# From the tenth tile on: attention scores in 64x32 sub-arrays without masked blocks, and the state's output of even and odd heads side by side

## The chip, the cores and the metric

One NeuronCore of one Trainium2 chip runs the whole program. TensorE does the matmuls (it writes PSUM, which has eight banks), VectorE, ScalarE and GpSimd do element-wise work, SyncE issues most DMAs. The metric is the device time of one execution in microseconds; the time before is the median of three runs, 780.83 us (778.70 to 780.98).

## The reference

Three parts in a row, for 4 batches, 8 heads, 768 steps and head size 48. First a linear attention with a decaying state, for each batch and head:

```
cur   = outer(u * k[t], v[t])
y[t]  = r[t] @ (state + cur)
state = w[t][:, None] * state + outer(k[t], v[t])
```

Its output, 3072 tokens of 384 features (8 heads of 48), goes through a feed-forward layer of width 2048, `(h * clip(h + 3, 0, 6) / 6) @ w_out` with `h = x @ w_in`, and then through a second one of width 1024, whose middle is `h * softmax(h)` followed by a normalisation. All inputs are float32.

## The kernel before, in words

Attention is cut into 24 tiles: 6 groups of 128 steps times 4 batches. Within a tile the recurrence is written as matmuls: running products of w (`q` backwards, `e` forwards) scale k and r. The scores of a tile are 128x128 for each head; only the part with the key's step before the query's step counts. The diagonal is replaced by `d`, the sum of r, k and u over the head. A tile goes through five stages, each with a function:

- `stw` clips w. `st0` brings w and r to the layout "head features on partitions" and builds `q` and `e`. `st1` does the same for k and multiplies r, k and u on GpSimd. From tile 10 (`LATE`) the turning is done by VectorE (`flip`, L438) from tiles that the DMA has laid out (`load_late`); before, TensorE does it.
- `st2` (L554 to L576) turns the scaled keys back (`ktp`, copied to `ktok`), computes the scores (`pa0` for even heads, whose 48 features lie on partitions 0 to 47, `pa1` for odd heads, on partitions 64 to 111), and makes `am`: GpSimd writes the diagonal (L572), VectorE copies the scores in where the mask `causal` says so (L576).
- `st3` (L585 to L639) computes the addition to the state (`kv`), then the tile's output `yt`: `inter` (L600) is scaled r times the decayed state `sp` or `sr`, `intra` (L607) is scores times v. Four matmuls of 32 output columns stand beside each other in the array. Features are stored as three chunks of 128: chunk c < 2 holds features 0 to 31 of heads 4c to 4c+3, chunk 2 the features 32 to 47 of all heads. VectorE adds `kv` to the state (L626), ScalarE and VectorE split the output into two float32r parts, `xh` (L638) and `xl` (L639).

The first feed-forward layer runs group by group, in 96 slots (6 groups times 16 blocks of its width). Slot n does `ffn_in(n)` (L657, nine matmuls into `h`), then the attention stages that are due, then `ffn_out(n - 2)` (L677, nine matmuls into three banks that are kept for the group). Each product is three float32r matmuls (hi*hi, hi*lo, lo*hi). ScalarE and VectorE do the function between (L661 to L665). `sched` sets the slots: for tile i from 10 on, with 4(i-4) as base, stages `stw` to `st2` stand in slots base-5 to base-2 and `st3` in base+2. So `st2` of tile i+1 and `st3` of tile i fall into the same slot, `st2` first. The second layer (L872 to L902) follows when the first is done.

PSUM: pool `ps_h` has two banks, for `h` and, from tile 9 on, `kv`; `ps_y` has three, for the feed-forward's sum; `ps_a` has three, through which the turned w, r, k, `ktp`, `pa0`, `pa1` and `yt` rotate (`ps_tile`). The order on SyncE is written out by hand; that of the other engines is set by a planner, which goes by program order and by when it thinks that operands and buffers are ready. Each engine then works in that order, and waits on semaphores.

Of the kernel before, what the change touches and what calls it, by code (L numbers as in the profile page):

```python
# [8 lines left out]
F32 = mybir.dt.float32  # L9
BF16 = mybir.dt.bfloat16  # L10
F32R = mybir.dt.float32r
I32 = mybir.dt.int32
# [6 lines left out]
P = 128  # L19
# [259 lines left out]
def fast_path(  # L279
# [70 lines left out]
    ps_a = right.enter_context(tc.tile_pool(name="ps_a", bufs=3, space=PSUM, side="right"))  # L350

    WN = KD * P + DM
    w1_h = w1p.tile([P, M1, WN], F32R, name="w1_h")
# [3 lines left out]
    def w1_load(m):  # L357
        ms = slice(m * P, (m + 1) * P)
        t = dec.tile([P, WN, 2], I32, tag="raw", name="raw", bufs=3)
        rows = w_in1[:, 2 * m * P:2 * (m + 1) * P]  # L360
        lo = t[:, 0:2 * P, :].rearrange("p (c f) w -> p c (f w)", c=2)
        src = rows.rearrange("(c q e) f -> c q e f", c=2, e=D)
# [46 lines left out]

    def late_open():  # L410
        pool = right.enter_context(tc.tile_pool(name="late", bufs=1, side="right"))
        for nm in ("w", "r", "k"):
# [3 lines left out]
            late[nm] = t  # L416

    def load_late(i):

        g, b = divmod(i, B)  # L420
        at[i] = {}
        for nm, src in (("w", w), ("r", r), ("k", k)):
            x = src[b].rearrange("(hp two) (n p j) d -> two n p hp (j d)", two=2, n=NG, j=4)
            for par in range(2):
                for half in range(2):
                    lo, n = 32 * half, 4 * D - 16 - 16 * half
                    o = 64 * par + lo
                    nc.sync.dma_start(out=late[nm][o:o + 32, :, 0:n], in_=x[par, g, :, :, lo:lo + n])
        for nm, src in (("r", r), ("k", k)):
            t = inp.tile([P, H, D], F32, tag=nm, name=nm)  # L430
            nc.sync.dma_start(out=t, in_=src[b, :, g * C:(g + 1) * C, :].rearrange("h t d -> t h d"))
            at[i][nm] = t
        load_v(i)

    def flip(nm):

# [5 lines left out]
        return t  # L442

    def ps_tile(nm):
        return ps_a.tile([P, 4, P], F32, tag="pa", name=nm)

    def ps_in(i, nm, spare):
        if i >= B:
# [94 lines left out]
        )  # L543
        a["sp"], a["sr"] = sp, sr

    def st2(i):
        a = at[i]
        g = i // B
        kq = a["q"][:, :, 1:C + 1]
        rr = a["e"]  # L550
        if g < NG - 1:
            ktp = ps_tile("ktp")
            for hp in range(HP):
                nc.tensor.transpose(out=ktp[:, hp, 0:DP], in_=kq[0:DP, hp, :], identity=ident[0:DP, 0:DP])  # L554
            ktok = atp.tile([P, HP, DP], F32, tag="ktok", name="ktok")
            nc.scalar.activation(out=ktok, in_=ktp[:, :, 0:DP], func=ACTF.Copy)
            a["ktok"] = ktok
        a["am"] = []
        pas = [ps_tile("pa0"), ps_tile("pa1")]
        d = atp.tile([P, H], F32, tag="d", name="d")  # L560
        nc.vector.tensor_reduce(out=d, in_=a["z"], axis=AX.X, op=ALU.add)
        for j in range(HP):
            for hh, pa in enumerate(pas):
                o = 64 * hh
                nc.tensor.matmul(
                    out=pa[:, j, :], lhsT=kq[o:o + D, j, :], rhs=rr[o:o + D, j, :], start=True, stop=True
                )
        dv = d.rearrange("p (j hh) -> p hh j", hh=2)
        for hh, pa in enumerate(pas):
            am = atp.tile([P, 4, C], F32, tag="am", name="am")  # L570
            a["am"].append(am)
            nc.gpsimd.tensor_tensor(  # L572
                out=am, in0=ident.unsqueeze(1).to_broadcast([P, HP, C]),
                in1=dv[:, hh, :].unsqueeze(2).to_broadcast([P, HP, C]), op=ALU.mult,
            )
            nc.vector.copy_predicated(am, causal.unsqueeze(1).to_broadcast([P, HP, C]), pa)  # L576

    def st3(i):
        a = at[i]
        g, b = divmod(i, B)  # L580
        if g < NG - 1:
            kv = ps_tile("kv") if i < JOIN - 1 else ps_h.tile([P, HP, P], F32, tag="h", name="kv")
            for h in range(H):
                o = 64 * (h % 2)
                nc.tensor.matmul(  # L585
                    out=kv[o:o + D, h // 2, 0:D], lhsT=a["ktok"][:, h // 2, o:o + D], rhs=a["v"][:, h, :],
                    start=True, stop=True, skip_group_check=True,
                )
        y = ps_tile("yt")

        def inter(c, first):
            for q in range(4):
                if c < 2:
                    h = 4 * c + q
                    hp, f = h // 2, D * (h % 2)
                    lhs = a["sp"][0:DP, hp, f:f + 32]
                else:
                    hp = q
                    lhs = a["sr"][0:DP, q, :]
                nc.tensor.matmul(  # L600
                    out=y[32 * q:32 * q + 32, c, :], lhsT=lhs, rhs=a["e"][0:DP, hp, :], start=first, stop=not first,
                    skip_group_check=True,
                )

        def intra(c, heads, lo, n, first, last):
            for q, h in enumerate(heads):
                nc.tensor.matmul(  # L607
                    out=y[32 * q:32 * q + n, c, :], lhsT=a["v"][:, h, lo:lo + n], rhs=a["am"][h % 2][:, h // 2, :],
                    start=first, stop=last, skip_group_check=True,
                )  # L610

        for c in range(2):
            if g > 0:
                inter(c, True)
            intra(c, range(4 * c, 4 * c + 4), 0, 32, g == 0, True)
        intra(2, range(1, H, 2), 16, 32, True, False)
        intra(2, range(0, H, 2), 32, 16, True, g == 0)
        if g > 0:
            inter(2, False)
        if g < NG - 1:  # L620
            for j in range(2):
                o, f = 64 * j, D * j
                dst = s_st[b][o:o + D, :, f:f + D]
                src = kv[o:o + D, :, 0:D]
                if g > 0:
                    nc.vector.tensor_tensor(out=dst, in0=src, in1=a["sp"][o:o + D, :, f:f + D], op=ALU.add)  # L626
                else:
                    nc.scalar.activation(out=dst, in_=src, func=ACTF.Copy)
        at.pop(i)
# [7 lines left out]
        xf = y[:, 0:KD, :]  # L637
        nc.scalar.activation(out=xh[:, :, sl], in_=xf, func=ACTF.Copy, accum_out=chk[:, 3 * i + 2:3 * i + 3])  # L638
        nc.vector.tensor_tensor(out=xl[:, :, sl], in0=xf, in1=xh[:, :, sl].bitcast(F32), op=ALU.subtract)  # L639

    stages = [stw, st0, st1, st2, st3]

# [50 lines left out]
    def range_a():  # L693

        xs = chk[:, 0:3 * NTILE].rearrange("p (n c) -> p n c", c=3)[:, :, 2]
        nc.vector.tensor_scalar(out=xs, in0=xs, scalar1=0.0, scalar2=None, op0=ALU.mult)
# [118 lines left out]
    for n in range(NSLOT + LAG):  # L815
        if n < NSLOT:
            ffn_in(n)
        for i, s in sorted(sched.get(n, []), key=lambda x: (x[0] - 2 * (x[0] >= JOIN and x[1] == 3), x[1])):
            stages[s](i)
            if s == NS - 1 and JOIN <= i + 1 < NTILE:  # L820
# [13 lines left out]
        if n == M1:  # L834
            dec_st.close()
            late_open()
        if n == NA:
# [127 lines left out]
```

## Time and profile before

| | |
|---|---|
| median of 3 runs | 780.83 us |
| the profiled execution | 780.79 us |
| its span in the profile | 779.1 us |
| TensorE matmul busy | 736.6 us (95%) |
| VectorE, ScalarE, GpSimd busy | 531.6, 333.6, 262.0 us |

The profile is of one execution. Busy time counts the time in which an engine has at least one instruction under way; TensorE's matmuls overlap, so the sum of their durations is larger than their share of the time, and what one costs in a run is read from the distance between starts. The page counts an fp32 matmul as two matmul instructions and a float32r matmul as one.

### The profile page before, as it was taken

What the parts mean: (1) busy time and instruction counts of PE and PEld (TensorE: products, weight loads), DVE (VectorE), ACT (ScalarE), POOL (GpSimd) and SP (SyncE); (2) the same over time, 40 slices, a digit from 0 to 9 for tenths busy, and PEclk for the clock granted to TensorE, in tenths of its full rate; (3) what the DMA queues carried; (4) which work ended last, traced back from release to release, by engine and by line L of the source; (5) the groups of instructions that cost most, each with busy time, mean ns of one, the idle gap of its engine ahead of it and who ended that gap; (6) DMA issues with size and microseconds to landing.
All of it is one profiled execution on the core that took longest, in us unless ns stands there. A gap on an engine that the chain in (4) does not pass through costs nothing. (4 is left out here: it accounts for less than half of the span.)

```text
span 779.1 us, 13589 instructions
## 1 busy us (share of the span) xinstructions
PE 736.6 (95%) x5084; PEld 621.3 (80%) x5084; DVE 531.6 (68%) x1010; ACT 333.6 (43%) x647; POOL 262.0 (34%) x355
## 2 busy tenths in 40 slices
PE   6669798999999999999999999999999999999996
PEld 4547676888888888888888887877889999999996
DVE  6989889667677777777778856886565555555552
ACT  3455555334444334433344335654444344333442
POOL 5566647642333233333233211232222222222200
PEclk8889997999999999999999999999999999999999
DMA  9785653514345333433334003440111111111001
GB/s 172 176 167 138 163 131 97 108 41 86 84 85 126 84 84 85 125 85 85 85 89 120 1 1 104 145 133 26 61 42 42 51 41 41 48 45 42 31 20 36
DMA packets 139435, 64.79 MB, mean 83 GB/s; under 512 B 90848, under 2 KB 133984, under 8 KB 139360
## 3 DMA queue, kind: packets, MB, share of 16 engines
q1 hardware_dynamic: 136768, 59.11, 32.2%
q10 hardware_dynamic: 2592, 4.72, 1.6%
q8 instruction: 42, 0.69, 0.4%
q14 instruction: 33, 0.27, 0.1%
HBM read 54.37 MB, written 9.44 MB: 82 GB/s over the span
## 5 line engine op out<-in xcount | busy, mean ns | idle before, releaser
L677 PE MATMUL y<-gh,w_h 128*128 128x512 f32 x288 | 116.7, 405 | 1.0 <-ACT ye L683 1.0
L657 PE MATMUL h<-xh,w_h 128*128 128x512 f32 x288 | 113.0, 393 | 3.0 <-DVE t L662 2.9
L677 PE MATMUL y<-gl,w_h 128*128 128x512 f32 x288 | 114.0, 396 | 0.0
L677 PE MATMUL y<-gh,w_l 128*128 128x512 f32 x288 | 113.4, 394 | 0.0
L657 PE MATMUL h<-xl,w_h 128*128 128x512 f32 x288 | 112.8, 392 | 0.0
L657 PE MATMUL h<-xh,w_l 128*128 128x512 f32 x288 | 112.5, 391 | 0.0
L661 ACT ACTIVATE t<-h,cols 128x512 f32<-128x512 f32 x96 | 65.3, 681 | 104.9 <-PE h L657 101.8
L663 ACT ACTIVATE gh<-t 128x512 fp32r<-128x512 f32 x96 | 60.5, 630 | 103.7 <-DVE t L662 103.5
L662 DVE SCALAR_TENSOR_TENSOR t<-t,h 128x512 f32<-128x512 f32 x96 | 65.4, 681 | 41.2 <-ACT t L661 41.0
L665 DVE TENSOR_TENSOR gl<-t,gh 128x512 fp32r<-128x512 f32 x80 | 66.8, 835 | 36.0 <-ACT gh L663 35.0
L78 DVE TENSOR_REDUCE nm<-h 128x1 f32<-128x1024 f32 x24 | 29.4, 1226 | 61.5 <-PE h L872 61.4
L899 PE MATMUL po<-w_oh,qh 128*128 128x384 f32 x192 | 67.1, 350 | 0.3 <-ACT qh L888 0.3
L657 PEld LDWEIGHTS h<-xh,w_h 128*128 128x128 f32 x288 | 54.4, 189 | 16.0 <-DVE t L662 4.2
L677 PEld LDWEIGHTS y<-gh,w_h 128*128 128x128 f32 x288 | 54.7, 190 | 15.5 <-issue 3.2
L899 PE MATMUL po<-w_oh,ql 128*128 128x384 f32 x192 | 64.7, 337 | 0.1
L899 PE MATMUL po<-w_ol,qh 128*128 128x384 f32 x192 | 64.8, 337 | 0.0
L677 PEld LDWEIGHTS y<-gh,w_l 128*128 128x128 f32 x288 | 54.9, 191 | 11.8
L677 PEld LDWEIGHTS y<-gl,w_h 128*128 128x128 f32 x288 | 55.0, 191 | 11.0 <-DVE gl L665 0.6
L657 PEld LDWEIGHTS h<-xh,w_l 128*128 128x128 f32 x288 | 54.4, 189 | 11.3
L657 PEld LDWEIGHTS h<-xl,w_h 128*128 128x128 f32 x288 | 54.4, 189 | 11.2
L888 ACT ACTIVATE qh<-pt 128x512 fp32r<-128x512 f32 x48 | 26.1, 597 | 78.3 <-PE pt L886 78.3
L872 PE MATMUL h<-w_ih,yl 128*128 128x512 f32 x144 | 56.4, 391 | 0.0
(123 smaller groups left out, 1478.7 us busy)
## 6 DMA issues: line engine op xcount, KB each, us to landing
raw<-in_moe_w_out_dram SPq DMA_DIRECT2D x24, 384.0 KB, 5.9
raw<-in_moe_w_in_dram SPq DMA_DIRECT2D x48, 128.0 KB
r<-in_r_dram SPq DMA_DIRECT2D x24, 192.0 KB
k<-in_k_dram SPq DMA_DIRECT2D x24, 192.0 KB, 3.7
v<-in_v_dram SPq DMA_DIRECT2D x24, 192.0 KB, 4.0
y1d<-ye ACTq DMA_DIRECT2D x18, 256.0 KB, 2.3
y<-y1d SPq DMA_DIRECT2D x24, 192.0 KB, 2.8
out_dram<-os SPq DMA_DIRECT2D x24, 192.0 KB, 1.9
```

The source lines that it names most:

```text
L78: nc.vector.tensor_reduce(out=nm, in_=h, axis=AX.X, op=ALU.max, negate=True)
L657: nc.tensor.matmul(out=h, lhsT=a, rhs=b, start=(j == 0), stop=(j == len(ops) - 1))
L661: nc.scalar.activation(out=t, in_=h, func=ACTF.Relu, bias=three)
L662: nc.vector.scalar_tensor_tensor(out=t, in0=t, scalar=6.0, in1=h, op0=ALU.min, op1=ALU.mult)
L663: nc.scalar.activation(out=gh, in_=t, func=ACTF.Copy)
L665: eng.tensor_tensor(out=gl, in0=t, in1=gh.bitcast(F32), op=ALU.subtract)
L677: nc.tensor.matmul(out=y_ps[g][c], lhsT=a, rhs=b, start=(m == 0 and j == 0), stop=(m == M1 - 1 and j == 2))
L872: nc.tensor.matmul(out=h[:, fs], lhsT=a[:, c, :], rhs=b_[:, c, fs], start=(j == 0), stop=(j == len(ops) - 1))
L888: nc.scalar.activation(out=qh[:, ms, :], in_=pt, func=ACTF.Copy)
L899: nc.tensor.matmul(out=po, lhsT=x[:, m, :], rhs=y[:, m, :], start=(n == 0), stop=(n == 3 * M2 - 1))
```

## The change

The scores leave `st2`: `keys_in` (turning the keys) stays there, while from tile 10 (`JOIN`) on `scores(i + 1)` is called in `st3(i)`, between the state addition and the output of tile i, so that the scores stand next to the part of the output that has the same array shape.

```
        else:
            mask, diag = late["mask"], late["diag"]
            d0 = d
            d = late["v"].tile([P, H], F32, tag="dt", name="dt")
            nc.gpsimd.tensor_copy(out=d[:, 0:4], in_=d0[:, 0:4])
            for o, n, t0 in turned:
                nc.gpsimd.tensor_copy(out=d[o:o + n, 4:8], in_=d0[t0:t0 + n, 4:8])
            for j in (0, 2, 1, 3):
                for x in range(4):
                    ks = 32 * x
                    for hh, pa in enumerate(pas):
                        o, p = 64 * hh, ks if j < 2 else 96 - ks
                        nc.tensor.matmul(
                            out=pa[p:p + 32, j, ks:C], lhsT=kq[o:o + D, j, ks:ks + 32], rhs=rr[o:o + D, j, ks:C],
                            start=True, stop=True, skip_group_check=True,
                        )
```

Each head's 128 keys are cut into four blocks of 32, and block x is multiplied only with the queries from step 32x on: 128, 96, 64 and 32 columns. For the head pairs j = 2 and 3 the blocks are stored in reversed order of partitions. So the mask, the diagonal, `d` and v are needed in that order for these heads: mask and diagonal are loaded once (`late_mask`), v once more for each tile in five DMAs (`load_turned`, tile `vt`), `d` by five small GpSimd copies.

```
+            mask, diag = (x.unsqueeze(1).to_broadcast([P, HP, C]) for x in (causal, ident))
...
+    turned = [(32 * q, 32, 96 - 32 * q) for q in range(4)]
+        for hs, parts in ((slice(0, 4), [(0, P, 0)]), (slice(4, 8), turned)):
+            for o, n, t0 in parts:
+                nc.sync.dma_start(out=t[o:o + n, hs, :], in_=src[hs, t0:t0 + n, :].rearrange("h t d -> t h d"))
```

The output's chunks 0 and 1 now hold features 0 to 31 of the even and of the odd heads (for all tiles; the rows of the feed-forward's weights are loaded in that order). From tile 10 on `inter` of chunk 0 takes 48 rows from partition 0, of chunk 1 48 rows from partition 64, both at the head, and chunk 1 goes to a bank of its own from `ps_h`:

```
+        if i >= JOIN:
+            y1 = ps_h.tile([P, C], F32, tag="h", name="yt1")
+            ys[1] = y1
...
+                    if i >= JOIN:
+                        rows = slice(64 * c, 64 * c + D)
+                    lhs = a["sp"][rows, q, D * c:D * c + 32]
...
+        if i >= JOIN:
+            inter(0, True)
+            inter(1, True)
...
+                (slice(1, 2), ys[1].unsqueeze(1), late["tot"][:, i:i + 1]),
+                (slice(0, KD, 2), y[:, 0:KD:2, :], chk[:, 3 * i + 2:3 * i + 3]),
```

`xh` and `xl` of these tiles are each made in two instructions. PSUM is divided anew in slot 22: `ps_a` is closed, two banks become `pa0` and `pa1` for good (cleared once, since the masked blocks are never written), one bank serves the turned w, r, k and `yt`. `ktp` of tiles from 10 on goes to `ps_h`, which then serves `h`, `ktp`, `kv` and `yt1`.

```
+    def ps_late():
+        ps_st.close()
+        pool = right.enter_context(tc.tile_pool(name="ps_s", bufs=1, space=PSUM, side="right"))
+        late["pa"] = [pool.tile([P, HP, C], F32, name=f"late_pa{j}") for j in range(2)]
+        for t in late["pa"]:
+            nc.vector.memset(t, 0.0)
+        late["one"] = right.enter_context(tc.tile_pool(name="ps_one", bufs=1, space=PSUM, side="right"))
...
+        if n == 4 * (JOIN - B) - 2:
+            ps_late()
+        if n >= max(LAG, 4 * (JOIN - B) - 2):
+            ffn_out(n - LAG)
         for i, s in sorted(sched.get(n, []), key=lambda x: (x[0] - 2 * (x[0] >= JOIN and x[1] == 3), x[1])):
...
-        if n >= LAG:
+        if LAG <= n < 4 * (JOIN - B) - 2:
             ffn_out(n - LAG)
```

So from slot 22 on `ffn_out` stands between `ffn_in` and the attention stages. In `st3` VectorE's additions to the state come ahead of the output, for all tiles.

## Rows read from the trace of the kernel before

**Rows 1.** The page: busy us (share of the span) and instructions.
```profile
PE 736.6 (95%) x5084; PEld 621.3 (80%) x5084; DVE 531.6 (68%) x1010; ACT 333.6 (43%) x647; POOL 262.0 (34%) x355
```
**Rows 2.** Stretches: length, busy of each engine, granted clock, DMA share, GB/s.
```profile
120.00:140.00 20.00, 17.33 (x76) 13.81 (x75) 16.64 (x28) 8.26 (x16) 13.22 (x12) 0.81 0.41 86
140.00:160.00 20.00, 20.00 (x170) 16.49 (x170) 12.88 (x25) 8.88 (x16) 13.72 (x20) 1.00 0.38 82
...
300.00:320.00 20.00, 20.00 (x165) 16.64 (x164) 14.44 (x29) 7.80 (x15) 6.44 (x8) 1.00 0.38 82
...
480.00:500.00 20.00, 19.03 (x85) 15.42 (x84) 15.61 (x27) 13.69 (x31) 5.55 (x6) 1.00 0.47 145
```
**Rows 3.** Waits of TensorE, 200 to 480 us: total us, times, longest.
```profile
PEld y L677 <- issue: 2.8, 14, 0.2
PEld pa L565 <- issue: 1.4, 4, 0.4
```
**Rows 4.** TensorE in order of time: start us, length us, operation, count.
```profile
300.59 0.39 PE L677 MATMUL y<-gh,w_h 128*128 128x512 f32 x1
...
304.67 0.39 PE L677 MATMUL y<-gh,w_h 128*128 128x512 f32 x1
...
306.71 0.39 PE L657 MATMUL h<-xh,w_h 128*128 128x512 f32 x1
...
308.52 0.40 PE L657 MATMUL h<-xh,w_l 128*128 128x512 f32 x1
308.76 0.55 PE L554 MATMUL ktp<-ident,q 112*128 112x112 f32 x4
309.23 1.16 PE L565 MATMUL pa<-e,q 48*128 48x128 f32 x16
310.32 0.56 PE L585 MATMUL kv<-v,ktok 128*48 128x48 f32 x16
310.82 0.42 PE L600 MATMUL yt<-e,sp 112*32 112x128 f32 x8
311.06 0.41 PE L607 MATMUL yt<-am,v 128*32 128x128 f32 x8
...
312.16 0.41 PE L600 MATMUL yt<-e,sr 112*32 112x128 f32 x8
312.50 0.50 PE L677 MATMUL y<-gh,w_h 128*128 128x512 f32 x1
312.83 0.40 PE L677 MATMUL y<-gl,w_h 128*128 128x512 f32 x1
```
**Rows 5.** The same view, from 310.815 to 310.85 us alone.
```profile
310.82 0.32 PE L600 MATMUL yt<-e,sp 112*32 112x128 f32 x4
```
**Rows 6.** Stretches (columns of rows 2): kv, and the output.
```profile
310.32:310.82 0.50, 0.50 (x18) 0.44 (x17) 0.10 (x1) 0.36 (x1) 0.00 (x0) 1.00 0.00 0
310.82:312.50 1.68, 1.68 (x61) 1.48 (x57) 1.33 (x4) 0.27 (x1) 0.00 (x0) 1.00 0.00 0
```
**Rows 7.** VectorE in order of time, about the same tile.
```profile
309.74 0.69 DVE L662 SCALAR_TENSOR_TENSOR t<-t,h 128x512 f32<-128x512 f32 x1 [0.95 <-ACT t L661]
...
311.73 0.72 DVE L626 TENSOR_TENSOR s_st<-kv,sp 48x192 f32<-48x192 f32 x2
...
316.10 0.54 DVE L639 TENSOR_TENSOR xl<-yt,xh 128x384 fp32r<-128x384 f32 x1
```
**Rows 8.** ScalarE in order of time.
```profile
309.60 0.54 ACT L556 ACTIVATE ktok<-ktp 128x448 f32<-128x448 f32 x1
```
**Rows 9.** GpSimd in order of time; in brackets the idle time before, and its cause.
```profile
312.59 0.84 POOL L535 TENSOR_TENSOR sp<-s_st,q 112x384 f32<-112x384 f32 x1 [2.95 <-PE yt L600]
...
315.39 0.41 POOL L539 TENSOR_TENSOR sr<-s_st,q 112x128 f32<-112x128 f32 x1
315.86 0.11 POOL L498 MEMSET q<- 112x4 f32 x1
```
**Rows 10.** The page: DMA issues, KB each, median us from issue to landing.
```profile
v<-in_v_dram SPq DMA_DIRECT2D x24, 192.0 KB, 4.0
```

More of the change, by code (lines that the diff above doesn't have):

```diff
@@ L349, in fast_path @@
     dec = dec_st.enter_context(tc.tile_pool(name="dec", bufs=2, side="right"))
-    ps_a = right.enter_context(tc.tile_pool(name="ps_a", bufs=3, space=PSUM, side="right"))
+    ps_st = ExitStack()
+    ps_a = ps_st.enter_context(tc.tile_pool(name="ps_a", bufs=3, space=PSUM, side="right"))
     WN = KD * P + DM
@@ L416, in late_open, with late_mask, load_turned @@
             late[nm] = t
+        late["tot"] = pool.tile([P, NTILE], F32, name="late_tot")
+        nc.gpsimd.memset(late["tot"], 0.0)
+        late["mask"] = pool.tile([P, HP, C], I32, name="late_mask")
+        late["diag"] = pool.tile([P, HP, C], F32, name="late_diag")
+    def late_mask(nm, src):
+        for hs, parts in ((slice(0, 2), [(0, P, 0)]), (slice(2, 4), turned)):
+            for o, n, t0 in parts:
+                nc.sync.dma_start(
+                    out=late[nm][o:o + n, hs, :], in_=src[t0:t0 + n, :].unsqueeze(1).to_broadcast([n, 2, C])
+                )
+    turned = [(32 * q, 32, 96 - 32 * q) for q in range(4)]
+    def load_turned(t, src):
+        for hs, parts in ((slice(0, 4), [(0, P, 0)]), (slice(4, 8), turned)):
+            for o, n, t0 in parts:
+                nc.sync.dma_start(out=t[o:o + n, hs, :], in_=src[hs, t0:t0 + n, :].rearrange("h t d -> t h d"))
     def load_late(i):
@@ L432, in load_late @@
             at[i][nm] = t
-        load_v(i)
+        if g < NG - 1:
+            load_v(i)
+        t = late["v"].tile([P, H, D], F32, tag="vt", name="vt")
+        load_turned(t, v[b, :, g * C:(g + 1) * C, :])
+        at[i]["vt"] = t
     def flip(nm):
@@ L544, in state_in, with keys_in @@
         a["sp"], a["sr"] = sp, sr
-    def st2(i):
+    def keys_in(i):
         a = at[i]
-        g = i // B
+        if i // B == NG - 1:
+            return
+        kq = a["q"][:, :, 1:C + 1]
+        ktp = ps_tile("ktp") if i < JOIN else ps_h.tile([P, HP, P], F32, tag="h", name="ktp")
+        for hp in range(HP):
+            nc.tensor.transpose(out=ktp[:, hp, 0:DP], in_=kq[0:DP, hp, :], identity=ident[0:DP, 0:DP])
+        ktok = atp.tile([P, HP, DP], F32, tag="ktok", name="ktok")
+        nc.scalar.activation(out=ktok, in_=ktp[:, :, 0:DP], func=ACTF.Copy)
+        a["ktok"] = ktok
@@ L549, in st2, with scores @@
+    def scores(i):
+        a = at[i]
         kq = a["q"][:, :, 1:C + 1]
         rr = a["e"]
[L551 to L557, printed above, removed]
         a["am"] = []
-        pas = [ps_tile("pa0"), ps_tile("pa1")]
+        pas = [ps_tile("pa0"), ps_tile("pa1")] if i < JOIN else late["pa"]
@@ L560, in st2 @@
         d = atp.tile([P, H], F32, tag="d", name="d")
         nc.vector.tensor_reduce(out=d, in_=a["z"], axis=AX.X, op=ALU.add)
[L562 to L567, printed above, removed]
+        if i < JOIN:
+            mask, diag = (x.unsqueeze(1).to_broadcast([P, HP, C]) for x in (causal, ident))
+            for j in range(HP):
+                for hh, pa in enumerate(pas):
+                    o = 64 * hh
+                    nc.tensor.matmul(
+                        out=pa[:, j, :], lhsT=kq[o:o + D, j, :], rhs=rr[o:o + D, j, :], start=True, stop=True
+                    )
+        else:
+            mask, diag = late["mask"], late["diag"]
[7 more added lines that the diff above has]
+                    ks = 32 * x
+                    for hh, pa in enumerate(pas):
+                        o, p = 64 * hh, ks if j < 2 else 96 - ks
+                        nc.tensor.matmul(
+                            out=pa[p:p + 32, j, ks:C], lhsT=kq[o:o + D, j, ks:ks + 32], rhs=rr[o:o + D, j, ks:C],
+                            start=True, stop=True, skip_group_check=True,
+                        )
@@ L579, in st3 @@
         a = at[i]
         g, b = divmod(i, B)
[L581 to L588, printed above, removed]
+        if g == NG - 1:
+            return
@@ new lines, in state_add @@
+        kv = ps_tile("kv") if i < JOIN - 1 else ps_h.tile([P, HP, P], F32, tag="h", name="kv")
+        for h in range(H):
+            o = 64 * (h % 2)
+            nc.tensor.matmul(
+                out=kv[o:o + D, h // 2, 0:D], lhsT=a["ktok"][:, h // 2, o:o + D], rhs=a["v"][:, h, :],
+                start=True, stop=True, skip_group_check=True,
+            )
+        for j in range(2):
+            o, f = 64 * j, D * j
+            dst = s_st[b][o:o + D, :, f:f + D]
+            src = kv[o:o + D, :, 0:D]
+            if g > 0:
+                nc.vector.tensor_tensor(out=dst, in0=src, in1=a["sp"][o:o + D, :, f:f + D], op=ALU.add)
+            else:
+                nc.scalar.activation(out=dst, in_=src, func=ACTF.Copy)
@@ L600, in inter, with intra @@
                 nc.tensor.matmul(
-                    out=y[32 * q:32 * q + 32, c, :], lhsT=lhs, rhs=a["e"][0:DP, hp, :], start=first, stop=not first,
+                    out=ys[c][32 * q:32 * q + 32, :], lhsT=lhs, rhs=a["e"][rows, q, :], start=first, stop=not first,
                     skip_group_check=True,
                 )
-        def intra(c, heads, lo, n, first, last):
-            for q, h in enumerate(heads):
+        def intra(c, par, lo, n, first, last):
+            for q in range(4):
@@ L614, in st3 @@
                 inter(c, True)
-            intra(c, range(4 * c, 4 * c + 4), 0, 32, g == 0, True)
-        intra(2, range(1, H, 2), 16, 32, True, False)
-        intra(2, range(0, H, 2), 32, 16, True, g == 0)
+            intra(c, c, 0, 32, g == 0, True)
+        intra(2, 1, 16, 32, True, False)
+        intra(2, 0, 32, 16, True, g == 0)
         if g > 0:
             inter(2, False)
[L620 to L628, printed above, removed]
@@ L629, in st3 @@
-        at.pop(i)
         if b == 0:
```

55 lines of the change are left out of this document (38 added, 17 removed).

## The prediction

> **What bounds the kernel now.** I read the page's busy shares first, then a table of 20 us stretches, then who waited for whom, then single stretches in order of time. TensorE's matmul row is busy 95% of the span [rows 1]. A mean over stages with different limits does not say where, so the table by stretch comes next: up to about 140 us TensorE has holes (17.33 of 20 us) and its granted clock is below full, from 140 us on it is busy 20.00 of 20 us at clock 1.00, and from 480 us it has small holes again [rows 2]. In the full stretch VectorE is busy 14.44 of 20 us, ScalarE 7.80, GpSimd 6.44. A busy share can hide short stalls, so the waits decide: between 200 and 480 us TensorE's waits are put down to "issue" (2.8 us in 14 times and 1.4 us in 4, [rows 3]), none to another engine. So a microsecond taken off TensorE there is a microsecond off the time, as long as no wait takes its place; the work after 480 us starts that much earlier and keeps its shape.
>
> The order of time shows the pitch [rows 4]. Eighteen feed-forward matmuls start from 300.59 to 304.67: 4.08 us, 0.227 each, 2.04 for the nine of an ffn_in or ffn_out. Between 308.76 and 312.50 stands one tile of attention: keys turned round (ktp) 0.47, scores (pa) 1.09, state addition (kv) 0.50, output (yt) 1.68 us. The first feed-forward matmul after it holds the engine 0.33 instead of 0.227, so a tile costs 3.74 + 0.11 = 3.85 us. The change touches pa and yt of 14 tiles (10 to 23), 2.77 us each.
>
> **The unit prices.** The page counts two matmul instructions for each fp32 matmul (x16 for 8 scores), two passes. In the output five groups of eight start from 311.06 to 312.16: 0.22 each [rows 4]. Eight instructions are four 32-column tiles times two passes, so the four run beside each other and a pass of 128 columns takes 0.110 us. Scores now: 4 head pairs x 2 passes x 0.110 = 0.88 for each half of the rows, the two halves beside each other; the remaining 0.21 of 1.09 is the change of array shape, draining and loading 128 columns of weights. kv has eight passes of 48 columns per half in 0.50 with about 0.14 of such loss, so 0.045 a pass. The line through 0.110 at 128 and 0.045 at 48 columns gives 0.084, 0.058 and 0.032 for 96, 64 and 32. The output's first group takes 0.24 instead of 0.22: loading 32 columns costs 0.02. The end of it, 312.16 + 0.22 to 312.50, leaves about 0.1 for draining; I use 0.09.
>
> **The change, part by part.**
> *Scores.* 32 matmuls (64 instructions) replace 8 (16). In 64x32 tiles there are eight sub-arrays: two row halves by four column strips. Per head pair each half has blocks of 128, 96, 64 and 32 columns, and the reversed pairs put the long block where the other pair had the short one. Lower bound, all sub-arrays always busy: 128 + 32 twice, or 96 + 64 twice, is 320 columns x 2 passes x 0.110/128 = 0.55 us. Upper bound of this mechanism, each pass waiting for its longest block: 0.88, as now. I take matmuls starting in program order, eight tiles in one pass, then their second pass. First pass of a pair: 0.110, for its long block opens the second. Of the second, the strip with 32 columns is free after 0.032 plus six starts of other tiles; four matmuls start within the 0.03 us up to 310.85 [rows 5], 0.007 each, so 0.032 + 0.042 = 0.074; there the next pair's long block goes in. (0.110 + 0.074) x 4 = 0.74, about 0.77 with the last tail. I use 0.75.
> *State's output side by side.* Even and odd heads used all 112 rows one after the other: 4 passes, 0.44. Now each uses 48 rows in its own row half and its own PSUM bank: two passes and eight more starts, 0.22 + 0.04 = 0.26. The bounds are 0.22 and 0.44.
> *Switches.* Before: ktp-pa-kv-yt-feed-forward, four. After: ktp-kv-(scores and state's output, one shape)-rest of yt-feed-forward, four. The last group's tiles have no ktp and kv: three and three.
> Sum of a tile: before 1.09 + 1.68 = 2.77. After: 0.02 + 0.75 + 0.26 + 0.09 = 1.12, and the rest of the output 1.68 - 4 x 0.11 = 1.24; together 2.36. Saved 0.41, times 14: 5.7 us.
>
> **What it adds elsewhere, and its cover.** *Banks.* ktp, kv and the odd heads' output now share ps_h's two banks with h. Count from T, the start of a slot's ffn_in (306.71 in the rows). ffn_out now comes ahead of the stages, so ktp starts at T + 4.08, kv at 4.55. kv needs h's bank, free when L662 ends (309.74 + 0.69, T + 3.72, [rows 7]): margin 0.8. The odd output needs ktp's bank, after ktok's copy on ScalarE, 0.54 [rows 8], behind gh: T + 5.2, wanted at about 5.8. The next h wants kv's bank at 7.5; the two additions (0.72 together) follow gl and end near 5.8. The h after that wants the odd output's bank 4.1 us after the tile's end; today xl ends 316.64 - 312.41 = 4.2 after it [rows 7], behind two predicated copies. Those hang on GpSimd's sp (312.59, [rows 9]), which can now start before the intra matmuls. I charge nothing; without that cover it is 0.1 to 0.5 a tile, at most 7 us.
> *One bank for the turned w, r, k and yt* (three banks rotated before, two of which held scores). The turnings, scans and products between are all VectorE's, in order: no new wait, but the product with k comes later in that order. Cost 0; VectorE's idle 5.5 of 20 us is the cover, and past it ktp would wait.
> *VectorE, ScalarE, GpSimd.* xl and xh are split: about 0.2 and 0.4 us more a tile, in engines with 5.5 and 12 us idle of 20. Five small GpSimd copies at 0.11 (the memset, [rows 9]) to 0.41 are 0.6 to 2 us in 13 idle; GpSimd waits for TensorE 2.95 us ahead of sp, and am is read 16 us later. Zero.
> *DMA.* Five issues and 192 KB more a tile. The issue of vt waits on SP for the output of the tile two before, about one slot; it stands last in its load and SP has nothing behind it for four slots. DMA is busy 0.38 there [rows 2]; the v load lands in 4.0 us [rows 10]. Zero. The masks load once, four slots early.
> *Once.* Two memsets of banks at slot 22, bounded by 0 and two 128x512 operations at 0.69; nine ffn_out matmuls (2.04) stand ahead of them on TensorE. Tiles 0 to 9 keep their counts; VectorE's additions come earlier in the order, and where TensorE has holes that can move either way by about 1 us. I charge 0.4 for all of this.
> Total: -5.7 + 0.4 = -5.3. The profiled execution took 780.79 us (span 779.1 and 1.7 around it); the median of the three runs, 780.83, is the same. Forecast 775.5.
>
> **Rivals.**
> *Sub-arrays take their work independently* (A): a strip that is done starts its next block whatever stands ahead in the program. Scores 0.55, output unchanged, 0.2 a tile more: 772.7. For it: passes of different tiles start 7 ns apart instead of one after the other [rows 5]. Against: all of today's passes in a run are equally long, so no row shows one overtaking. The Trainium skill ("TensorE: Matmul & The Clock Gate", Part 3, The mechanism) says matmuls start and end in program order, only weight loads go ahead; by it the sum stays at 775.5. No run here shows unequal blocks.
> *The gain is mostly lost* (B): only four tiles are interleaved at a time, as in today's output. Then each four pay their first pass: scores about 0.94, state's output 0.37, saved 0.11 a tile, 1.5 us: 779.3. A bank wait of 0.3 us a tile comes to the same. For it: runs of four are the most that rows show; against: two and four tiles are each as many as the code offered.
> *Instruction starts become the bound* (C), the other side. The rows show bursts 7 ns apart, but no long run so dense. In kv 18 matmuls and 17 loads fall in 0.50 us, in the output 61 and 57 in 1.68 [rows 6]: 14 ns an instruction. kv's passes average 0.045/2 = 22.5 ns a matmul, the output's 27.5. The new run has 64 + 16 = 80 matmuls, at these spacings 1.8 to 2.2 us instead of 1.01. A tile then costs 0.11 + 1.8 (2.2) + 1.24 = 3.15 (3.55) against 2.77: 5.3 to 10.9 us slower, 786 to 792. It decides above (2.77 - 1.24 - 0.11)/80 = 18 ns a matmul. Against it: both spacings are explained by columns alone (48 and 128), so they are ceilings on the spacing, not floors. The Trainium skill ("TensorEngine Tiling (Array Packing)", Instruction Overhead) speaks for C: it puts about 60 cycles on each matmul and advises not to take a tiling factor from a dimension already small. By its figure, as an estimate at 2.4 GHz, 80 x 25 ns are 2.0 us, inside C; kv's 22.5 ns lies just below it, which argues against it as a floor, narrowly.
>
> **Chances.** Forecast 0.48, A 0.18, B 0.17, C 0.17. A measurement of this kernel tells about 0.3% from no change, 2.3 us. Faster by more (below 778.5): A, nearly all of the forecast, a little of B: 0.66. Within: most of B and a few of the forecast's stalls: 0.18. Slower: C less its mild end: 0.16. The forecast's own range is 773.5 to 778; with A below and B and unforeseen stalls above, 771.8 to 783, which leaves out C and a little of A.
>
> **What would show it.** Right: pa's 64 instructions span 0.7 to 0.8 us from first to last start, the two sp groups together 0.25 to 0.3, a tile from ktp to the first feed-forward matmul about 3.3 instead of 3.74, waits of TensorE between 200 and 480 us still "issue" alone. A shows as scores near 0.55, B as near 0.95, C as starts spaced evenly near 20 ns whatever the block. Wrong elsewhere: TensorE waiting for kv, yt1 or h on VectorE or ScalarE once a tile, or a different start of the full stretch.

## The result: 1% slower, and the profile after

The changed kernel takes 788.86 us (median of 6 runs, 784.83 to 790.62), the kernel before 780.90 beside it: a ratio of 1.0105, interval 1.0074 to 1.0136. The forecast was 775.5 with a range up to 783.0, so it was wrong in sign. The profiled execution took 789.40 us.

Two lines of the page, the span and the busy row that answers to [rows 1]:

```profile
span 787.7 us, 15130 instructions
...
PE 742.0 (94%) x5756; PEld 620.5 (79%) x5756; DVE 527.6 (67%) x1027; ACT 337.3 (43%) x675; POOL 270.3 (34%) x426
```

TensorE has 672 matmul instructions more (14 tiles of 48) and is busy 5.4 us longer, which says nothing of where the time went. The starts of the 96 slots (the first `h` matmul of each) do. Differences of the two profiled executions, one of each kernel, after less before:

```
start to slot 22           +0.60
slots 22 to 81 (14 tiles)  +1.16   = 14 x -0.20, and +4.0 of stalls in slots 34, 50, 54, 66
slots 82 to 87             +0.67   (slot 82: 5.34 -> 5.99)
slots 88 to 94             +3.93   (32.79 -> 36.72)
slot 95 to the last matmul -0.01
last matmul to the end     +2.26   (6.76 -> 9.02, from its start)
span                       +8.6    (779.1 -> 787.7)
```

So the tiles did become shorter, by half of what was predicted, and the rest is lost in four places outside the scores. First a tile, TensorE in order of time (start, length, operation, count), which answers to [rows 4]:

```profile
291.44 0.55 PE L588 MATMUL ktp<-ident,q 112*128 112x112 f32 x4
291.96 0.56 PE L642 MATMUL kv<-v,ktok 128*48 128x48 f32 x16
292.46 1.00 PE L621 MATMUL late_pa<-e,q 48*32 48x128 f32 x64
293.22 0.59 PE L674 MATMUL yt<-e,sp 48*32 48x128 f32 x16
293.75 1.08 PE L681 MATMUL yt<-am,vt 128*32 128x128 f32 x32
294.64 0.40 PE L674 MATMUL yt<-e,sr 112*32 112x128 f32 x8
294.98 0.50 PE L742 MATMUL h<-xh,w_h 128*128 128x512 f32 x1
```

From start to start: keys turned 0.52, kv 0.50, scores 0.76, state's output side by side 0.53, the rest 1.23; 3.54 in all against 3.74 [rows 4]. The scores came out as forecast (0.75). The state's output did not: 0.53 against 0.26 and 0.09 for draining. The starts of single matmuls, in ns after 292.459, taken from the trace's records, show why:

```
scores, first 8 : 0 7 14 20 27 34 40 47
then, to the 32nd: 93 99 107 114 120 124 127 131 134 140 163 ... 259 265 271 278
the next ones    : 320 429 438 454 471 488 504 521 538 559 565 ... 733
state's output   : 765 772 873 874 889 905 906 923 939 956 1004 1021 1037 1054 1070 1087
```

Up to the 32nd instruction sub-arrays take work as they come free, and out of program order (the second pass of the block with 32 columns starts at 93, that of the block with 128, ahead of it in the program, at 124). From 438 to 538 there is one start every 16.6 ns, whatever the columns; from 559 to 733 the starts are denser (23 of them); the state's output has one or two a step of 16.6 ns for most of its run. Over all 80 instructions the mean is 13.8 ns. Each of these matmuls has a weight load of its own, and the loads fall into the same steps (450, 467, 484, 500, 517, 534 ns), so the rows don't tell whether the load, the matmul or the pair sets the step; "instructions" below stands for the pair.

Next the waits of TensorE's weight loads, then of its matmuls, 200 to 490 us (total us, times, longest), beside [rows 3]:

```profile
PEld y L762 <- ACT ye L768: 6.4, 8, 1.2
...
PEld kv L642 <- DVE t L747: 1.9, 7, 0.8
```
```profile
PE y L762 <- ACT ye L768: 2.8, 6, 0.8
PE kv L642 <- DVE t L747: 0.6, 1, 0.6
```

`ye` (L768) is ScalarE's copy of a finished group's sum out of its three banks. Slot 66 (408.48) in order of time, ScalarE and TensorE:

```profile
410.22 0.66 ACT L746 ACTIVATE t<-h,cols 128x512 f32<-128x512 f32 x1
...
410.79 1.07 ACT L768 ACTIVATE ye<-y 128x512 f32<-128x512 f32 x2
...
411.42 0.50 PE L762 MATMUL y<-gh,w_h 128*128 128x512 f32 x1 [0.74 <-ACT ye L768]
...
412.55 0.60 ACT L768 ACTIVATE ye<-y 128x512 f32<-128x512 f32 x1 [0.17 <-ACT gh L748]
...
413.20 0.50 PE L762 MATMUL y<-gh,w_h 128*128 128x512 f32 x1
```

The new group's first `y` comes right behind `ffn_in` now and finds the banks still full; before, the tile's attention stood between (3.7 us, in the last group 2.9). Slots 34, 50 and 66 are 1.02, 0.89 and 1.45 us longer than the normal ones for it; slot 54 is 0.65 longer, where kv waited for its bank. The last is no fixed cost: in e2 and e5 below, where VectorE, ScalarE and GpSimd have the same order up to slot 66, slot 54 takes 7.62 and 7.65 instead of 8.28.

The late stretch: TensorE by stretch of time (length, busy, instructions, granted clock, DMA share, GB/s); slots 90, 92, 93:

```profile
521.75:527.86 6.11, 4.25 (x19) 1.00 0.34 116
...
532.21:536.00 3.79, 2.60 (x11) 1.00 0.18 52
536.00:538.00 2.00, 1.34 (x6) 1.00 0.34 98
538.00:540.00 2.00, 2.00 (x7) 0.50 0.00 0
540.00:542.00 2.00, 2.00 (x7) 0.64 0.00 0
542.00:544.31 2.31, 2.31 (x11) 1.00 0.04 7
```

The same columns in the kernel before, slots 91 and 92:

```profile
523.32:529.56 6.24, 4.67 (x19) 1.00 0.45 133
529.56:533.88 4.32, 4.32 (x19) 1.00 0.26 76
```

VectorE and TensorE of the kernel after in the middle of it, in order of time:

```profile
532.07 1.18 DVE L834 TENSOR_SCALAR dec<-dec,gcol 128x384 f32<-128x384 f32 x1
...
533.17 0.66 DVE L66 TENSOR_SCALAR raw<-raw 128x384 int32<-128x384 int32 x1
...
534.66 0.55 DVE L50 SCALAR_TENSOR_TENSOR dec<-dec,raw 128x384 int32<-128x384 int32 x1
...
535.13 1.48 DVE L750 TENSOR_TENSOR gl<-t,gh 128x512 fp32r<-128x512 f32 x1
...
536.66 0.50 PE L762 MATMUL y<-gl,w_h 128*128 128x512 f32 x1 [1.85 <-DVE gl L750]
```

VectorE still decodes the second layer's weights (`raw`, `dec`) where the first layer wants `gl` of it. TensorE waits 1.85 us, and then its granted clock falls from 1.00 to 0.50 (2.4 to 1.2 GHz) for 3.4 us: slot 93 takes 5.18 instead of 4.08. In the kernel before the clock is 1.00 through slots 88 to 94.

How much this stretch costs differs from execution to execution. In e9 below, the changed kernel with a few DMAs more at its start and the same late order, TensorE waits 1.89 us at the same place, but the clock stays at 1.00, and slots 88 to 94 take 34.42 us: 1.6 more than before, not 3.9.

The end: TensorE's last matmul before (span 779.1), then TensorE's last matmul and ScalarE's last copy after (span 787.7).

```profile
772.32 0.34 PE L899 MATMUL po<-w_oh,ql 128*128 128x384 f32 x1
```

```profile
778.68 0.34 PE L993 MATMUL po<-w_oh,ql 128*128 128x384 f32 x1
779.19 0.58 ACT L996 ACTIVATE os<-po,st 128x384 f32<-128x384 f32 x1 [4.60 <-PE po L993]
```

SyncE's own records show what follows: a branch at 780.79, nothing for 2.85 us, one semaphore instruction, nothing for 2.23 us, then the closing sequence. The kernel before has one such gap (2.67 us).

### The profile page after: what moved, and what is told of

Read it like the earlier page. It is cut to its first block, busy times and chain, and to the rows that moved or that the text cites. A ratio compares the mean times of both kernels' runs of the same rounds, so it can differ in the third digit from the quotient of the medians.

```text
span 787.7 us, 15130 instructions
## 1 busy us (share of the span) xinstructions
PE 742.0 (94%) x5756; PEld 620.5 (79%) x5756; DVE 527.6 (67%) x1027; ACT 337.3 (43%) x675; POOL 270.3 (34%) x426
## 5 line engine op out<-in xcount | busy, mean ns | idle before, releaser
L742 PE MATMUL h<-xh,w_h 128*128 128x512 f32 x288 | 115.6, 402 | 2.9 <-DVE t L747 2.9
L750 DVE TENSOR_TENSOR gl<-t,gh 128x512 fp32r<-128x512 f32 x80 | 57.3, 716 | 30.1 <-ACT gh L748 28.8
L762 PEld LDWEIGHTS y<-gl,w_h 128*128 128x128 f32 x288 | 55.0, 191 | 13.8 <-DVE gl L750 3.1
```

The lines of the kernel that those rows point to most:

```text
L742: nc.tensor.matmul(out=h, lhsT=a, rhs=b, start=(j == 0), stop=(j == len(ops) - 1))
L750: eng.tensor_tensor(out=gl, in0=t, in1=gh.bitcast(F32), op=ALU.subtract)
L762: nc.tensor.matmul(out=y_ps[g][c], lhsT=a, rhs=b, start=(m == 0 and j == 0), stop=(m == M1 - 1 and j == 2))
```

## The experiments

Each ratio is to the kernel before, measured beside it on the same chip (its medians: 780.45 us for e1 to e4, 780.79 for e5 to e7, 780.93 for e8 to e10). Stretches are of one profiled execution each, and the start of slot 22, which most edits don't touch, lies between 184.1 and 188.0 us in the twelve profiles; so slots are compared, not spans.

**e1_tot_left: the second sum of checks in another pool.** The check of the output's range reads `late_tot`, which lay in a pool that must close before the second layer's weights are loaded.

```
-        late["tot"] = pool.tile([P, NTILE], F32, name="late_tot")
+        keep = left.enter_context(tc.tile_pool(name="late_t", bufs=1, side="left"))
+        late["tot"] = keep.tile([P, NTILE], F32, name="late_tot")
```

> The sums of tile 10 on (late_tot) lie in a pool that stays open instead of one that closes in slot 78. Theory R (release): the first load of the second layer's weights waits for the read of late_tot, because its memory is only free then; it is issued 7.1 us after slot 78 begins (4.0 before the change), and the decoding that starts late runs into the feed-forward in slots 88 to 94, which are 3.9 us longer than before. Expected: issue at 5.5 to 6 us after the slot's begin, slots 88 to 94 shorter by 1 to 2.5 us, time 786.5 to 788. Rival (overlap of VectorE and GpSimd by chance): the issue moves, the slots stay as long, 788.9.

Measured: 785.17 us, 1.0060 [1.0046, 1.0074]. In the kernel after, SyncE's queue waited for that check (first view, 440 to 500 us), and the first load went out at 474.25 (second view, SyncE in order of time), 7.14 us into slot 78 against 4.04 before:

```profile
SPq L810 <- DVE chk L781: 35.6, 1, 35.6
```
```profile
474.25 0.39 SPq L810 DMA_DIRECT2D gcol<-in_moe_g_ln_dram  x1
```

In e1:

```profile
471.21 0.38 SPq L811 DMA_DIRECT2D gcol<-in_moe_g_ln_dram  x1
```

That is 6.0 us into slot 78, and the wait in slot 82 is gone (4.08 us). But slots 88 to 94 still take 36.60 us. The late load was not their cause. Slots 82 to 87 are 1.7 us shorter than in the kernel after; another 1.9 of this profile's 4.0 us lies before slot 22, where no row ties it to the edit.

**e2_ffn_last_66: e1, and `ffn_out` back behind the stages from slot 66 on.**

```
-        if n >= max(LAG, 4 * (JOIN - B) - 2):
+        first = 4 * (JOIN - B) - 2 <= n < 4 * (NTILE - 2 * B)
+        if first:
             ffn_out(n - LAG)
```

> As e1_tot_left, and ffn_out goes back behind the attention stages from slot 66 on (where no kv is computed). Theory R: the first weight load is issued about 4 us after slot 78 begins, and slots 88 to 94 come back to their length before the change, -3.9 us. Theory Y (ffn_out in front leaves ScalarE only ffn_in's 2 us to empty the three sum banks at a group's end): slot 66, 8.13 us long, becomes about 6.8, -1.4 us; slots 34 and 50 stay long. Both: 783 to 784. Rival: a stall of another cause, no shorter than e1_tot_left.

Measured: 783.40 us, 1.0031 [1.0018, 1.0045]. Slot 66 falls from 8.12 to 6.93, but most of it comes back two slots later, where the next `h` waits for its bank and slot 68 takes 5.09:

```profile
PEld h L743 <- DVE t L748: 1.3, 1, 1.3
```

Slots 66 to 69 together are only 0.14 shorter (20.49 in e1, 20.35 here). Slots 88 to 94 fall to 32.11, as short as before the change. So the time met its 783 to 784, but the 1.4 us expected of slot 66 are not in it. TensorE's waits of 485 to 550 us:

```profile
PE h L743 <- DVE t L748: 2.5, 2, 1.6
PE y L763 <- ACT ye L769: 0.8, 1, 0.8
```

What differs is VectorE's order. In the kernel after and in e1 the last tile's `xl` and the checks behind it run in slot 79 and decoding begins in slot 80; in the kernel before and in e2 they run in slot 78 and decoding begins in slot 79. By the end of slot 91 VectorE has done 55 of the 56 decoding steps (`raw` and `dec`) before and in e2, 52 in after and in e1; of the other four, two then stand ahead of `gl` in slot 92 and two ahead of the next `t`. e9 has the late order too (52 steps). So `ffn_out`'s place decides this order and with it a loss in slots 88 to 94; its size is 3.9, 3.8 and 1.6 us in the three profiles with `ffn_out` in front to the end (after, e1, e9), against -1.0 to +0.9 in the eight others.

**e3_state_in_turn: e2 with the state's output as before.** 112 rows, chunk after chunk, one bank, `xh` and `xl` whole.

```
-                    if i >= JOIN:
-                        rows = slice(64 * c, 64 * c + D)
...
-        if i >= JOIN:
-            inter(0, True)
-            inter(1, True)
```

> As e2_ffn_last_66, with the state's output as before the change (112 rows, even and odd in turn, one bank, one split). Theory S (instruction supply: after some 32 matmuls that stood ready, TensorE gets a load and a matmul every 16.6 ns, so 80 matmuls of scores and state's output take 1.09 us whatever their columns): side by side gains nothing; a tile from ktp to the next feed-forward matmul stays at 3.54 within 0.06, the time within 1 us of e2. Theory of the prediction (columns bound): 0.18 a tile longer, 2.5 us over e2.

Measured: 781.61 us, 1.0013 [1.0000, 1.0025]. TensorE in one tile:

```profile
353.18 1.00 PE L622 MATMUL late_pa<-e,q 48*32 48x128 f32 x64
354.11 0.43 PE L670 MATMUL yt<-e,sp 112*32 112x128 f32 x8
354.35 0.40 PE L677 MATMUL yt<-am,vt 128*32 128x128 f32 x8
354.57 0.40 PE L670 MATMUL yt<-e,sp 112*32 112x128 f32 x8
```

The slot of a tile with the one after it: 12.03 us before, 11.84 in after and e2, 11.88 in e3. Side by side is worth 0.04 a tile, not 0.18 (0.44 to 0.26). The forecast of the tile held, that of the time did not: it is 1.8 us below e2. In the profiles slots 34, 50 and 66 to 69 are 1.95 us shorter than in e2, so what comes with side by side there (a third user of `h`'s banks, `xh` and `xl` in two parts) cost more than it gave; which of these it was, no run separates.

**e4_masked_too: e2 with all 128 query columns in each block**, the masked ones too: as many instructions, more columns.

```
-    out=pa[p:p + 32, j, ks:C], lhsT=kq[o:o + D, j, ks:ks + 32], rhs=rr[o:o + D, j, ks:C],
+    out=pa[p:p + 32, j, :], lhsT=kq[o:o + D, j, ks:ks + 32], rhs=rr[o:o + D, j, :],
```

> As e2_ffn_last_66, but every block of 32 keys is multiplied with all 128 queries: 512 instead of 320 columns for each sub-array, as many instructions. Theory S: the 64 + 16 matmuls span 1.09 now; at 0.88 for the scores' columns the supply catches up and the state's output runs at column speed, so 1.1 to 1.2 in all, 0 to 1.5 us over e2. Columns bound: 0.33 a tile more, 4.6 us over e2.

Measured: 789.25 us, 1.0102 [1.0085, 1.0119]. One tile, and a wait of 200 to 490 us:

```profile
337.11 1.20 PE L622 MATMUL late_pa<-e,q 48*32 48x128 f32 x64
338.06 0.46 PE L675 MATMUL yt<-e,sp 48*32 48x128 f32 x16
338.45 1.10 PE L682 MATMUL yt<-am,vt 128*32 128x128 f32 x32
```
```profile
PE kv L643 <- DVE t L748: 3.2, 5, 1.1
```

Scores and state's output take 1.34 us (0.95 and 0.39) where e2 takes 1.29: 60% more columns (512 instead of 320 for a sub-array) cost 0.05 us a tile. That is what a limit on instructions gives: the scores take 0.16 longer, and the state's output, behind them, 0.11 shorter. The time, 5.9 us above e2, met neither forecast and is no measure of it: kv now waits for its bank on VectorE (3.2 us here), `h` for `xl` and `t` (2.5 us). Why these waits come with more columns is not shown.

**e5_one_more_dma: e2 with one DMA more on SyncE.**

```
-    nc.sync.dma_start(out=u_bc, in_=u.partition_broadcast(P))
+    for o in (0, P // 2):
+        nc.sync.dma_start(out=u_bc[o:o + P // 2], in_=u.partition_broadcast(P // 2))
```

> e2_ffn_last_66 with the load of u (spread over 128 partitions) cut in two halves of 64, so that SyncE has one DMA instruction more ahead of the end of the program; nothing else differs. Theory 'place of the code': in the changed kernel SyncE shows two gaps (2.85 and 2.23 us) in its last instructions, with one semaphore instruction between them, where the kernel before shows one (2.67 us); the second gap belongs to the place at which the last instructions lie, so one more instruction ahead moves it and the time from the last matmul to the end falls from 8.7 to about 6.5 us, 781.2 us in all. Rival 'work at the end': the 2.2 us belong to what the changed kernel adds (pools, semaphores to be cleared), then the end stays at 8.5 to 9.0 us and the time at 783.4 (within 0.5).

Measured: 781.58 us, 1.0009 [0.9997, 1.0022], near the expected number, but not by its reason: from the last matmul to the end it is 8.70 us still, with both gaps (2.50 and 2.26). SyncE has 636 recorded instructions as in e2, one DMA more and one wait fewer, so nothing moved. The profiled execution reached slot 22 at 184.1 instead of 186.8; with the load cut in eight (e9) it was 188.0, so this is the spread of runs rather than the split load.

**e6_blocks_of_64: e3 with blocks of 64 keys and the order of the kernel before.**

```
+    KB = 64
-                for x in range(4):
-                    ks = 32 * x
+                for ks in range(0, P, KB):
...
-        if i < JOIN:
-            scores(i)
+        scores(i)
...
-        if JOIN <= i + 1 < NTILE:
-            scores(i + 1)
         out_x(i)
+        if i >= JOIN:
+            state_add(i, a)
...
-        if n >= LAG and not first:
+        if n >= LAG:
             ffn_out(n - LAG)
```

> e3_state_in_turn with key blocks of 64 instead of 32 (64x64 sub-arrays, two blocks a head with 128 and 64 columns, pairs 2 and 3 reversed: 32 instructions and 384 columns for each of the four sub-arrays, instead of 64 instructions and 320 columns for each of eight), and with the order of the kernel before: scores in st2 ahead of the state addition, the addition to the state on VectorE behind the output, ffn_out last in every slot. Theory 'supply of instructions' (16.6 ns for each matmul with its weights where blocks are short): 32 x 16.6 = 0.53 us is below the columns' 384 x 2 passes x 0.110/128 = 0.66, so columns set it; scores 0.75 to 0.8 with the switch of shape against 0.93 in e3, so with scores 0.3 shorter than the 1.09 before a tile is 0.25 to 0.3 us below before's, and the waits for ScalarE in slots 34 and 50 go: 776 to 778 us. Rival 'columns alone': 384 against 320 columns would make the scores no shorter than in e3, and the time no lower than 780.

**e7_blocks_of_32: e6 with `KB = 32`.**

> e6_blocks_of_64 with blocks of 32, nothing else: 64 instructions for the scores instead of 32, 320 columns for each sub-array instead of 384. Theory 'supply of instructions': 64 x 16.6 = 1.06 less the first some 32 that stand in the queue, so about 0.9 to 0.95 with the switch, 0.15 us a tile more than e6_blocks_of_64, about 2 us in all, although a sub-array has fewer columns. Rival 'columns alone': 0.11 us a tile less than e6_blocks_of_64, about 1.5 us in all.

Measured: e6 779.82 us, 0.9988 [0.9972, 1.0003]; e7 781.31 us, 1.0006 [0.9993, 1.0020]. One tile of e6, then of e7:

```profile
349.06 0.90 PE L622 MATMUL late_pa<-e,q 48*64 48x128 f32 x32
349.89 0.42 PE L669 MATMUL yt<-e,sp 112*32 112x128 f32 x8
```
```profile
349.45 1.00 PE L622 MATMUL late_pa<-e,q 48*32 48x128 f32 x64
350.38 0.43 PE L669 MATMUL yt<-e,sp 112*32 112x128 f32 x8
```

Scores 0.83 against 0.93, the two slots 11.78 against 11.88, slots 22 to 81 295.59 against 296.99: half the instructions with a fifth more columns are faster, as the limit on instructions has it (0.10 a tile, 0.15 expected). No slot waits for `ye` between 30 and 78 in either. e6 missed its 776 to 778: its tiles' slots give 2.4 us against the kernel before, although slot 22 takes 8.61 instead of 7.96, but slots 82 to 94 take 1.3 of it back (slot 82: 5.77 instead of 5.34). It can't be told from the kernel before.

**e8_banks_earlier: e6 with PSUM divided in slot 21.**

```
-        if n == 4 * (JOIN - B) - 2:
+        if n == 4 * (JOIN - B) - 3:
             ps_late()
```

> e6_blocks_of_64 with PSUM divided anew in slot 21 instead of slot 22, nothing else. In e6_blocks_of_64 slot 22 takes 8.61 us where the following ones take 7.70, and TensorE waits there ahead of the scores (0.6 us put down to ScalarE's t, long done by then). Theory: the two clearings of the score banks stand on VectorE right ahead of the first scores; one slot earlier nothing waits for them, slot 22 falls to about 7.8 and the time to 779.0 or a little below (-0.8 us). Rival: the wait is for ktp's or the keys' chain on VectorE, then slot 22 stays at 8.6 and the time at 779.8.

Measured: 779.44 us, 0.9990 [0.9977, 1.0003]; slot 22 still 8.68, its wait now 0.71 us ahead of the turned keys, for VectorE's product `q`. The number is the rival's, but the edit did not do what it was meant to: VectorE still clears the banks in slot 22 (1.02 us, 2.1 us into the slot, 2.4 in e6), now ahead of the keys' chain. Whether the clearing costs slot 22 its 0.9 us stays open.

**e9_after_u_in_8: the changed kernel with seven DMAs more on SyncE.**

```
+    for o in range(0, P, 16):
+        nc.sync.dma_start(out=u_bc[o:o + 16], in_=u.partition_broadcast(16))
```

> The changed kernel itself with the load of u cut into 8 DMAs of 16 partitions, so seven DMA instructions more on SyncE ahead of its end (e5_one_more_dma had one more DMA but one wait fewer, 636 instructions as before it, so it moved nothing). Theory 'place of the code': the second gap (2.2 us) among SyncE's last instructions goes, the stretch from the last matmul to the end falls from 9.0 to about 6.8 us and the time from 788.9 to about 786.7. e6_blocks_of_64 (605 instructions) ends 6.8 and e7_blocks_of_32 (636) 8.7 us after the last matmul with the same end, which speaks for it. Rival 'work at the end': it stays at 8.5 to 9.0 and 788.9.

Measured: 786.99 us, 1.0093 [1.0072, 1.0114], 1.9 us below the changed kernel's median, which was taken with other runs of the kernel before beside it (780.90). The page's span and the last rows in order of time:

```profile
span 785.3 us, 15136 instructions
```
```profile
778.49 0.34 PE L994 MATMUL po<-w_oh,ql 128*128 128x384 f32 x1
779.00 0.58 ACT L997 ACTIVATE os<-po,st 128x384 f32<-128x384 f32 x1 [4.61 <-PE po L994]
```

6.79 us remain from the start of the last matmul, 2.2 fewer, and SyncE has one gap (2.76). Recorded SyncE instructions and that stretch: 562 and 6.76 (before), 605 and 6.78 (e6), 605 and 6.91 (e8), 642 and 6.79 (e9); 636 and 9.02 (after), 8.71 (e1), 8.70 (e2, e5), 8.82 (e3), 8.49 (e4), 8.69 (e7), 8.77 (e10). e7 differs from e6 in 32 small loads (of v and the masks) and the scores alone. So it goes with the number of SyncE's instructions, and so perhaps with where its last ones lie, not with what the change does at the end; why, no row shows. The two ratio intervals overlap, so the 2.2 us rest on the traces; and that the time met its forecast is in part luck, for this execution also began 1.9 us later than the changed kernel's and was 2.3 us shorter in slots 88 to 94.

**e10_short_columns: e7 with each block of 32 keys against its own 32 queries alone.**

```
-    out=pa[p:p + KB, j, ks:C], ... rhs=rr[o:o + D, j, ks:C],
+    out=pa[p:p + KB, j, ks:ks + KB], ... rhs=rr[o:o + D, j, ks:ks + KB],
```

> e7_blocks_of_32 with each block of 32 keys multiplied with 32 queries only, instead of up to 128: the same 64 instructions a tile with 160 columns less in each second block and 128 columns instead of 320 for a sub-array. It leaves out the scores of queries further than the block's own 32 steps. Theory 'supply of instructions': the run keeps its length, 0.9 us a tile with about 14 to 17 ns between starts, and the time stays within 1.5 us of e7_blocks_of_32 (780 to 781.3). Rival 'columns': 128/320 of the run, so about 0.35 to 0.4 with the switch of shape, 0.5 us a tile less and 7 us in all (774).

(A sub-array has 128 columns there instead of 320; the "160 in each second block" of that text is a slip.) Measured: 779.54 us, 0.9988 [0.9972, 1.0003].

```profile
348.58 0.76 PE L622 MATMUL late_pa<-e,q 48*32 48x32 f32 x64
349.27 0.43 PE L669 MATMUL yt<-e,sp 112*32 112x128 f32 x8
```

0.69 us: neither theory. From first to last start it is 0.56, where the columns alone would need 0.2 (seven passes of 0.03) and e7, with 320 columns, takes 0.73. The starts, in ns after the first: 32 instructions by 163, nothing until 241, then 281, 298, 314, 331, 348, 364, 381, 398 and so on to 565, mostly one or two instructions a step of 16.6 ns. So the limit on instructions is there with few columns too, and costs most of the 0.56; but columns add to it (0.73). "The run keeps its length" was too strong.

## Why the prediction was wrong

The forecast was 5.3 us less, the profiled span grew by 8.6. The 13.9 between them, by the prediction's own steps:

- *Scores, 0.75.* Right in size (0.76 in the tile shown), but by luck: its premise, work in program order, does not hold. The first 32 instructions behave as rival A has it, the others as rival C, and the two together happen to come near the sum.
- *State's output side by side, 0.26.* The step that failed inside the tile: 0.53 with draining against 0.35, and 0.05 more for the turned keys. It stands behind 64 instructions, past the 32 that start freely, and its own 16 come one or two a step of 16.6 ns: 0.32 from first to last start, where the sum had 0.15. I took runs with a burst of four [rows 5] and let 80 instructions follow each other like that. Rival C's mechanism was real, but the mean over its 80 instructions is 13.8 ns, below the 18 at which it would have decided: it halved the gain instead of reversing it. A tile saved 0.20 instead of 0.41, 14 of them 2.9 us less.
- *Moving `ffn_out` forward: "I charge nothing".* I counted `ps_h`'s banks with margins, and not those of `ps_y`, which the moved matmuls write. Every sixteenth slot they hold a finished group that ScalarE must copy out, and the attention stages had been the cover. Slots 34, 50 and 66 cost 3.4 us. e6 and e7, with `ffn_out` last in every slot, have no such wait up to slot 78; e2 takes the one in slot 66 away and has another for it in slot 68. Kv's wait in slot 54, 0.65, is of `ps_h`'s banks, and not in every execution. Slots 82 to 87, 0.67, go with the pool of `late_tot`: in e1, with `ffn_out` still in front, slot 82 has its 4.08. One wait of the kind stood in the trace of before, 1.0 us in slot 82 (the row below, of the waits from 60 to 560 us); the prediction argued from 200 to 480 us alone.

```profile
PE y L677 <- ACT ye L683: 1.0, 1, 1.0
```

- *"The work after 480 us starts that much earlier and keeps its shape."* It did not: 3.9 us in the profiled execution. `ffn_out` in front put the last tile's `xl` one slot later on VectorE, the decoding behind it too, and VectorE bounds slots 88 to 92. 1.1 of it is the granted clock of 0.50 that followed the idle time, which e9 did not have; there the loss is 1.6. e1 had excluded the later load as the cause.
- *"Once", 0.4.* The start is 0.6 longer, which the spread of runs covers (slot 22 began between 184.1 and 188.0 us in twelve profiles), the end 2.3, of which nothing in the profile of before gave a sign, and which e9 ties to the number of SyncE's instructions.

The chances were too sure of the cover: the 0.16 for slower held rival C alone. Of what came, a bank wait was named, but among `ps_h`'s banks and once a tile.

Two rules stood beside the prediction. The Trainium skill ("TensorE: Matmul & The Clock Gate", Part 3, The mechanism) has matmuls start in program order; the trace disagrees, for passes in other sub-arrays start ahead (93 before 124 ns above). The same section of the Trainium skill speaks of a reorder window 64 deep; by estimate 32 weight loads and 32 matmuls would fill it, which fits the border after the 32nd matmul, but no run here tests it. The Trainium skill ("TensorEngine Tiling (Array Packing)", Instruction Overhead) has about 60 cycles for each matmul, by estimate 25 ns at 2.4 GHz; the rows of e10 have 5.3 ns between starts for the first 32 instructions and 9.0 over all 64, so the figure is too high here, but its direction, not to cut a small dimension further, is what e6 against e7 shows.

## What to carry to other kernels

Cutting matmuls into sub-array blocks shortens a run as long as the instructions are few: here the scores took 1.09 us in 16 instructions on whole columns, 0.83 in 32 on 64x64 sub-arrays, and 0.93 in 64 on 64x32, although the columns fell each time (512, 384 and 320). When a step is moved ahead, look at the banks that it writes, and at every user of them that the old place had covered, above all at the rare one at a group's boundary. And compare the order on the second busiest engine: a stretch that it bounds later can inherit the shift, as slots 88 to 92 did.

## What the runs showed of the hardware

- Short matmuls in sub-arrays start out of program order, 5 to 9 ns apart on average, for 32 instructions; past these most starts come in steps of 16.6 ns, mostly one or two a step (after, e7, e10) with denser stretches between (after, 559 to 733 ns).
- TensorE's granted clock fell from 1.00 to 0.50 for 3.4 us after stretches in which it was busy 2.60 of 3.79 and 1.34 of 2.00 us (after, slots 92 and 93; e1 likewise). The kernel before, with waits up to 1.6 us in slots 89 to 91, kept 1.00, and so did e9 with the same wait of 1.9 us in slot 92 (4.52 of 6.41 us busy).
- The end of the program has a second gap of 2.0 to 2.3 us in the eight kernels with 636 recorded SyncE instructions, and not in the four with 562, 605 or 642.
